# One core, linear attention followed by a highway layer: tokens on partitions to the output, row sums and bias as products, one load form, and an order from a list scheduler

## The chip, the cores and the metric

The kernel runs on 1 core of one Trainium2 chip. The metric is the device time in microseconds; the time before is the median of 3 runs. All reads and writes of HBM, the preparation of the weights and the whole computation lie inside it.

## What is computed

Inputs are q, k and v, each 8 batches x 8 heads x 576 positions x 64 values in float32 (9.4 MB each), two weight matrices of 512 x 512, and a bias of 512. The output is 4608 x 512 in float32 (9.4 MB).

```python
q_s = exp(q - max(q, -1)); q_s /= sum(q_s, -1)        # softmax over the 64 values of a head
k_s = exp(k - max(k, 2));  k_s /= sum(k_s, 2)         # softmax over the 576 positions
kv  = einsum('bhsd,bhse->bhde', k_s, v)               # 64 x 64 for each head
x   = einsum('bhsd,bhde->bhse', q_s, kv)              # then (batch, position) x (head, value) = 4608 x 512
H   = maximum(x @ w_h, 0)
T   = sigmoid(x @ w_t + b_t)
out = T * H + (1 - T) * x
```

Both kernels leave out the subtraction of the maxima: it cancels in the quotient, and the inputs are small (0.1 times a normal draw). Both write the sigmoid as a tanh, T = (1 + tanh(z/2)) / 2[...]. With that, out = x + (1 + tanh(z/2)) (H - x) / 2.

## The kernel before

Two stages run over 8 batches. Positions of a batch are split into a main part of 512 (4 positions on each of 128 partitions, runs of 1 KB in HBM) and a tail of 64 (one position on each of 64 partitions, runs of 256 B). Products have 16-bit inputs.

*Loads* (`load_batch`, L78 to L95). k and q come as float32 through the SyncE queue (L85, L86 and two tails). v comes through GpSimd's queue and is cast to 16 bits on the way: four transfers for the four positions of the main part (L88) and one for the tail (L91). The weights take the same way (L215, L216). Columns of ones are set beside v on VectorE (L92, L93). Each of these tiles has three buffers; batch b+2 is loaded at the end of batch b.

*Prelude* of a batch (L97 to L127). ScalarE takes exp of k and q, main part and tail. VectorE sums exp(q) over each head's 64 values (L112, L113), takes the reciprocal, and multiplies exp(q) by it (L120, L125), all on tiles of 128 x 2048 for the main part. The prelude of batch b+1 is written into batch b behind its first pair of heads.

*Attention*, by pairs of heads (L250 to L286, `flush_rb` L234 to L248). TensorE forms kv for each head of a pair from exp(k) and v, with a column of ones beside v that gives the column sums of exp(k). It transposes the normalised q into PSUM. VectorE takes the reciprocal of the column sums (L279), copies the two 64 x 64 blocks into a block-diagonal 128 x 128 tile (L281 to L283), and scales the transposed q on its way to SBUF (L285). A product (L239, tail L243) gives x with its 512 features on partitions and positions along the free axis; ScalarE copies it into `xT` (L247, L248), which holds all 4608 columns.

*Highway layer*, by chunks of 512 tokens and 128 features (`moe_dc`, L141 to L165). Four products accumulate x W_h and four x W_t, with the weights as the stationary operand. ScalarE takes the tanh, with the bias as a value per partition (L158). VectorE takes dd = max(h, 0) - x (L161), GpSimd uu = dd * tanh (L163), VectorE ww = uu + dd (L172) and gg = 0.5 ww + x (L174). Since features lie on partitions, gg has to be turned: `moe_finish` transposes it on TensorE (L73), ScalarE copies the result to float32 (L191), and the rows are stored through the SyncE queue (L199).

*Order.* The text of the loops sets it: in batch b, each pair of heads is followed by one `moe_dc` of token chunk b-1. Chunks 7 and 8 are done at the end. The tile framework places the waits and may move instructions within its rules; each engine then takes its instructions in a fixed order.

Of the kernel before, what the change touches and what calls it, by code (L numbers as in the profile page):

```python
# [8 lines left out]
FP32 = mybir.dt.float32  # L10
FP16 = mybir.dt.float16
AF = mybir.ActivationFunctionType
ALU = mybir.AluOpType


@with_exitstack
def kernel(
# [10 lines left out]
    nc = tc.nc  # L28
    B, H, S, D = q.shape
    NTOK = B * S  # L30
    DM = H * D
    P = 128
    SM = (S // P) * P
    ST = S - SM
    NPAIR = H // 2
    NJ = SM // P
    KC = DM // P
    assert 0 < ST <= 64

    q_m = q[:, :, 0:SM, :].rearrange("b h (p j) d -> b p h j d", p=P)  # L40
    k_m = k[:, :, 0:SM, :].rearrange("b h (p j) d -> b p h j d", p=P)
    v_m = v[:, :, 0:SM, :].rearrange("b h (p j) d -> b p h j d", p=P)
    q_t = q[:, :, SM:S, :].rearrange("b h p d -> b p h d")
    k_t = k[:, :, SM:S, :].rearrange("b h p d -> b p h d")
    v_t = v[:, :, SM:S, :].rearrange("b h p d -> b p h d")
    w_h_d = moe_w_h.rearrange("(c p) n -> p c n", p=P)
    w_t_d = moe_w_t.rearrange("(c p) n -> p c n", p=P)
    b_t_d = moe_b_t.rearrange("(c p) -> p c", p=P)

    def col_to_row(cg):  # L50
        b_ = cg // S
        u = cg % S
        if u < SM:
            return b_ * S + NJ * (u % P) + (u // P), NJ
        return b_ * S + u, 1

    consts = ctx.enter_context(tc.tile_pool(name="consts", bufs=1))
    xTp = ctx.enter_context(tc.tile_pool(name="xTp", bufs=1))
    qkv = ctx.enter_context(tc.tile_pool(name="qkv", bufs=3))
    ex = ctx.enter_context(tc.tile_pool(name="ex", bufs=2))  # L60
    at_s = ctx.enter_context(tc.tile_pool(name="at_s", bufs=3))
    mo = ctx.enter_context(tc.tile_pool(name="mo", bufs=3))
    gp = ctx.enter_context(tc.tile_pool(name="gp", bufs=5))
    og = ctx.enter_context(tc.tile_pool(name="og", bufs=3))
    ps_qt = ctx.enter_context(tc.tile_pool(name="ps_qt", bufs=2, space=bass.MemoryType.PSUM))
    ps_xt = ctx.enter_context(tc.tile_pool(name="ps_xt", bufs=1, space=bass.MemoryType.PSUM))
    ps_ht = ctx.enter_context(tc.tile_pool(name="ps_ht", bufs=3, space=bass.MemoryType.PSUM))
    ps_nat = ctx.enter_context(tc.tile_pool(name="ps_nat", bufs=2, space=bass.MemoryType.PSUM))

    xT = xTp.tile([P, KC, NTOK], FP16)  # L70

    def ptrans(out_ap, in_ap, idn):
        nc.tensor.matmul(  # L73
            out_ap, in_ap, idn, is_transpose=True, start=True, stop=True,
            skip_group_check=True,
        )

    def load_batch(b):  # L78
        q32m = qkv.tile([P, H, NJ, D], FP32, tag="q32m")
        k32m = qkv.tile([P, H, NJ, D], FP32, tag="k32m")  # L80
        v16m = qkv.tile([P, H, NJ, D + 8], FP16, tag="v16m")
        q32t = qkv.tile([ST, H, D], FP32, tag="q32t")
        k32t = qkv.tile([ST, H, D], FP32, tag="k32t")
        v16t = qkv.tile([P, H, D + 8], FP16, tag="v16t")
        nc.sync.dma_start(k32m, k_m[b])  # L85
        nc.sync.dma_start(q32m, q_m[b])  # L86
        for j in range(NJ):
            nc.gpsimd.dma_start(v16m[:, :, j, 0:D], v_m[b][:, :, j, :])  # L88
        nc.sync.dma_start(q32t, q_t[b])
        nc.sync.dma_start(k32t, k_t[b])  # L90
        nc.gpsimd.dma_start(v16t[0:ST, :, 0:D], v_t[b])  # L91
        nc.vector.memset(v16m[:, :, :, D : D + 8], 1.0)  # L92
        nc.vector.memset(v16t[0:ST, :, D : D + 8], 1.0)  # L93
        nc.vector.memset(v16t[ST:P, :, :], 0.0)
        return q32m, k32m, v16m, q32t, k32t, v16t  # L95

    def prelude(b):  # L97
        q32m, k32m, v16m, q32t, k32t, v16t = loaded[b]
        eq16m = ex.tile([P, H, NJ, D], FP16, tag="eq16m")
        eq16t = ex.tile([ST, H, D], FP16, tag="eq16t")  # L100
        ek16m = ex.tile([P, H, NJ, D], FP16, tag="ek16m")
        ek16t = ex.tile([P, H, D], FP16, tag="ek16t")
        nc.scalar.activation(ek16m, k32m, AF.Exp)  # L103
        nc.scalar.activation(ek16t[0:ST], k32t, AF.Exp)
        nc.scalar.activation(eq16m, q32m, AF.Exp)  # L105
        nc.scalar.activation(eq16t, q32t, AF.Exp)
        nc.vector.memset(ek16t[ST:P], 0.0)
        eqm_g = eq16m.rearrange("p h j d -> p (h j) d")
        qsm = at_s.tile([P, H * NJ], FP16, tag="qsm")
        qst = at_s.tile([ST, H], FP16, tag="qst")  # L110
        with nc.allow_low_precision("fp16 softmax denominators (64 summands)"):
            nc.vector.reduce_sum(qsm, eqm_g, axis=mybir.AxisListType.X)  # L112
            nc.vector.reduce_sum(qst, eq16t, axis=mybir.AxisListType.X)  # L113
        rqm = at_s.tile([P, H * NJ], FP32, tag="rqm")
        rqt = at_s.tile([ST, H], FP32, tag="rqt")
        nc.vector.reciprocal(rqm, qsm)
        nc.vector.reciprocal(rqt, qst)
        qs16m = ex.tile([P, H, NJ, D], FP16, tag="qs16m")
        qs16t = ex.tile([P, H, D], FP16, tag="qs16t")
        nc.vector.tensor_mul(  # L120
            qs16m.rearrange("p h j d -> p (h j) d"),
            eqm_g,
            rqm.broadcast_to([P, H * NJ, D]),
        )
        nc.vector.tensor_mul(qs16t[0:ST], eq16t, rqt.broadcast_to([ST, H, D]))  # L125
        nc.vector.memset(qs16t[ST:P], 0.0)
        return ek16m, ek16t, qs16m, qs16t  # L127

    moe_state = {}

    def moe_start(tcn):
        moe_state[tcn] = {
            "nat": [
                ps_nat.tile([P, 2 * DM], FP16, tag="nat", name=f"nat_{tcn}_{i}")
                for i in range(2)
            ],
            "gg": [],
            "pend": [],
        }

    def moe_dc(tcn, dc):  # L141
        st = moe_state[tcn]
        tok = slice(tcn * 512, (tcn + 1) * 512)
        dsl = slice(dc * P, (dc + 1) * P)
        psh = ps_ht.tile([P, 512], FP32, tag="ht")
        pst = ps_ht.tile([P, 512], FP32, tag="ht")
        for kc in range(KC):
            nc.tensor.matmul(  # L148
                psh, w16h[:, kc, dsl], xT[:, kc, tok],
                start=(kc == 0), stop=(kc == KC - 1),  # L150
            )
        for kc in range(KC):
            nc.tensor.matmul(  # L153
                pst, w16t[:, kc, dsl], xT[:, kc, tok],
                start=(kc == 0), stop=(kc == KC - 1),
            )
        th = mo.tile([P, 512], FP16, tag="th")
        nc.scalar.activation(th, pst, AF.Tanh, bias=bt2[:, dc : dc + 1], scale=0.5)  # L158
        xs = xT[:, dc, tok]
        dd = mo.tile([P, 512], FP16, tag="dd")  # L160
        nc.vector.scalar_tensor_tensor(dd, psh, 0.0, xs, op0=ALU.max, op1=ALU.subtract)  # L161
        uu = mo.tile([P, 512], FP16, tag="uu")
        nc.gpsimd.tensor_mul(uu, dd, th)  # L163
        moe_flush_pend(tcn)
        st["pend"].append((dd, uu, xs, dc))  # L165

    def moe_flush_pend(tcn):
        st = moe_state[tcn]
        while st["pend"]:
            dd, uu, xs, dc = st["pend"].pop(0)  # L170
            ww = mo.tile([P, 512], FP16, tag="ww")
            nc.vector.tensor_add(ww, uu, dd)  # L172
            gg = gp.tile([P, 512], FP16, tag="gg")
            nc.vector.scalar_tensor_tensor(gg, ww, 0.5, xs, op0=ALU.mult, op1=ALU.add)  # L174
            st["gg"].append((gg, dc))

    def moe_finish(tcn):
        st = moe_state.pop(tcn)
        nats = st["nat"]
        for gg, dc in st["gg"]:  # L180
            for t in range(4):
                ptrans(
                    nats[t // 2][
                        :, (t % 2) * DM + dc * P : (t % 2) * DM + (dc + 1) * P
                    ],
                    gg[:, t * P : (t + 1) * P],
                    ident,
                )
        for half in range(2):
            o32 = og.tile([P, 2, DM], FP32, tag="o32")  # L190
            nc.scalar.copy(o32.rearrange("p a b -> p (a b)"), nats[half])  # L191
            for tt in range(2):
                c0 = tcn * 512 + half * 256 + tt * P
                i = 0
                while i < P:
# [24 lines left out]
    for _ in range(34):  # L220
        ptrans(warm[:, 0:P].bitcast(FP16)[:, 0:P], ident, ident)
# [3 lines left out]
    for b in range(B):  # L225
        ek16m, ek16t, qs16m, qs16t = pre.pop(b)
        _, _, v16m, _, _, v16t = loaded[b]
        if b > 0:
            moe_start(b - 1)
# [109 lines left out]
```

The softmax here doesn't subtract the row's maximum and nothing guards it: scores larger than these inputs give would overflow.

## Time and profile before

| what | value |
|---|---|
| time, median of 3 runs | 222.03 us (221.61 to 222.95) |
| span of the profiled run | 219.1 us, 3271 instructions |
| HBM read, written | 30.41 MB, 9.44 MB |
| DMA packets | 69696, 34.29 MB as written |

The profile gives the busy time of each engine over the span, the same in 40 equal slices (a digit is tenths of a slice), the DMA queues, and the chain of work that ended last. "hardware_dynamic" is the queue of the transfers that SyncE issues, "software_dynamic" of those that GpSimd issues. Groups of instructions are given by line, engine, operation and shapes, with count, busy time and mean; then the idle time of the engine just before them and what ended it. Overlapping matmuls make TensorE's busy time an upper measure of its work. [...]

### The profile page before, as it was taken

The page shows a single profiled execution, that of the slowest core. Times are in us where ns is not written, and L with a number is a line of the kernel's source. Part 1 is how long each engine was busy: PE and PEld are TensorE (multiplying, and loading weights), DVE is VectorE, ACT ScalarE, POOL GpSimd, SP SyncE. Part 2 cuts the span into 40 slices and gives each one's busy share as a digit, 9 for nine tenths or more (in the row PEclk, how much of TensorE's full clock was granted, in tenths as well). Part 3 has the DMA queues.
Part 4 walks back from the last instruction along what each step waited for, and adds up shares of the span by engine and source line. Part 5 has one row for each costly group of instructions (what it writes and reads, how often), then busy time and mean ns, then how long its engine had stood idle before and what let it go on. Part 6 is the DMA issues. An engine that isn't in the chain of part 4 may idle for free.

```text
span 219.1 us, 3271 instructions
## 1 busy us (share of the span) xinstructions
PE 137.4 (63%) x1170; PEld 71.3 (33%) x1170; DVE 164.5 (75%) x357; ACT 102.0 (47%) x151; POOL 79.5 (36%) x84
## 2 busy tenths in 40 slices
PE   4110573029768553894799299939965899878420
PEld 4110441014334221542354045415522455334210
DVE  3074595009993899699979997999999999878820
ACT  2443344603676423783667464607532275535230
POOL 8532311231566304650294049222402434452600
PEclk9855558556999797699589959985996999999955
DMA  6999999999999999997899209920060033071426
GB/s 185 253 211 268 210 249 252 229 270 223 274 221 186 127 280 223 283 112 160 262 254 162 93 0 73 183 47 0 3 193 3 0 120 74 0 195 50 141 56 135
DMA packets 69696, 34.29 MB, mean 157 GB/s; under 512 B 47664, under 2 KB 65072, under 8 KB 69680
## 3 DMA queue, kind: packets, MB, share of 16 engines
q1 hardware_dynamic: 31120, 28.32, 50.4%
q0 software_dynamic: 38560, 5.77, 37.2%
q8 instruction: 9, 0.15, 0.3%
q14 instruction: 7, 0.06, 0.1%
HBM read 30.41 MB, written 9.44 MB: 182 GB/s over the span
## 4 chain that ended last, share of the span: by engine, by line
DVE 38%; DMA 30%; issue 13%; POOL 9%; PE 4%; ACT 2%; ACTq 1%; POOLq 0%; DVEq 0%
DMA v16m<-in_v_dram 30%; DVE gg L174 9%; POOL uu L163 5%; DVE dd L161 5%; DVE qsm L112 5%; DVE ww L172 5%; DVE qsT L285 4%; POOL v16m L88 3%; DVE qs16t L125 2%; DVE abk L283 2%; DVE qst L113 1%; DVE rz L279 1%; PE qtt L73 1%; DVE abk L282 1%; PE nat L73 1%
## 5 line engine op out<-in xcount | busy, mean ns | idle before, releaser
L163 POOL TENSOR_TENSOR uu<-dd,th 128x512 f16<-128x512 f16 x36 | 43.3, 1205 | 79.1 <-DVE dd L161 66.1
L153 PE MATMUL pst<-xT,w16t 128*128 128x512 f16 x144 | 44.8, 415 | 17.7 <-DVE dd L161 17.2
L148 PE MATMUL psh<-xT,w16h 128*128 128x512 f16 x144 | 42.2, 395 | 5.5 <-ACT th L158 3.5
L88 POOL DMA_DIRECT2D v16m<-in_v_dram x32 | 28.9, 906 | 37.1 <-DMA v16m<-in_v_dram 19.0
L158 ACT ACTIVATE th<-pst,bt 128x512 f16<-128x512 f32 x36 | 24.9, 691 | 32.5 <-PE pst L153 32.5
L174 DVE SCALAR_TENSOR_TENSOR gg<-ww,xT 128x512 f16<-128x512 f16 x36 | 34.8, 966 | 0.3
L247 ACT CAST xT<-pxT 128x512 f16<-128x512 f32 x32 | 18.7, 583 | 27.7 <-PE qtt L243 27.5
L260 PE MATMUL qtt<-v16m,ek16m 128*64 128x65 f16 x256 | 17.6, 224 | 22.2 <-DMA v16m<-in_v_dram 21.4
L260 PEld LDWEIGHTS <-ek16m 128*64 128x64 f16 x256 | 12.4, 129 | 41.3 <-issue 41.1
L112 DVE TENSOR_REDUCE qsm<-eq16m 128x32 f16<-128x2048 f16 x8 | 18.2, 2277 | 9.8 <-ACT eq16m L105 9.7
L172 DVE TENSOR_TENSOR ww<-uu,dd 128x512 f16<-128x512 f16 x36 | 18.7, 520 | 9.0 <-POOL uu L163 8.7
L153 PEld LDWEIGHTS <-w16t 128*128 128x128 f16 x144 | 13.7, 102 | 35.0 <-issue 23.7
L105 ACT ACTIVATE eq16m<-q32m 128x2048 f16<-128x2048 f32 x8 | 15.3, 1907 | 21.0 <-DMA q32m<-in_q_dram 9.3
L161 DVE SCALAR_TENSOR_TENSOR dd<-psh,xT 128x512 f16<-128x512 f32 x36 | 23.9, 664 | 1.1 <-PE psh L148 1.0
L73 PE MATMUL nat<-ident,gg 128*128 128x128 f16 x144 | 16.3, 245 | 12.8 <-DVE gg L174 12.5
L191 ACT CAST o<-nat 128x1024 f32<-128x1024 f16 x18 | 17.4, 1016 | 12.9 <-PE nat L73 12.9
L73 PE MATMUL qtt<-ident,qs16m 128*64 128x128 f16 x256 | 22.5, 258 | 0.0
L103 ACT ACTIVATE ek16m<-k32m 128x2048 f16<-128x2048 f32 x8 | 15.4, 1920 | 13.2 <-DMA k32m<-in_k_dram 12.6
L279 DVE RECIPROCAL rz<-qtt 128x1 f32<-128x1 f32 x32 | 5.2, 162 | 20.0 <-PE qtt L73 19.8
L239 PE MATMUL pxT<-qsT,abk 128*128 128x512 f16 x32 | 14.9, 465 | 6.5 <-ACT xT L247 3.7
L148 PEld LDWEIGHTS <-w16h 128*128 128x128 f16 x144 | 13.2, 100 | 17.3 <-issue 6.3
L285 DVE TENSOR_SCALAR qsT<-qtt,rz 128x640 f16<-128x640 f16 x32 | 17.6, 550 | 1.0
(38 smaller groups left out, 170.8 us busy)
## 6 DMA issues: line engine op xcount, KB each, us to landing
k32m<-in_k_dram SPq DMA_DIRECT2D x8, 1024.0 KB, 12.5
q32m<-in_q_dram SPq DMA_DIRECT2D x8, 1024.0 KB, 14.2
out_dram<-o SPq DMA_DIRECT2D x40, 128.0 KB, 2.4
v16m<-in_v_dram POOLq DMA_DIRECT2D x32, 128.0 KB, 10.2
out_dram<-o SPq DMA_DIRECT2D x16, 256.0 KB, 2.7
q32t<-in_q_dram SPq DMA_DIRECT2D x8, 128.0 KB, 11.4
k32t<-in_k_dram SPq DMA_DIRECT2D x8, 128.0 KB, 10.3
v16t<-in_v_dram POOLq DMA_DIRECT2D x8, 64.0 KB, 11.2
```

The lines of the kernel that those rows point to most:

```text
L73: nc.tensor.matmul(out_ap, in_ap, idn, is_transpose=True, start=True, stop=True, skip_group_check=True,)
L88: nc.gpsimd.dma_start(v16m[:, :, j, 0:D], v_m[b][:, :, j, :])
L112: nc.vector.reduce_sum(qsm, eqm_g, axis=mybir.AxisListType.X)
L148: nc.tensor.matmul(psh, w16h[:, kc, dsl], xT[:, kc, tok], start=(kc == 0), stop=(kc == KC - 1),)
L153: nc.tensor.matmul(pst, w16t[:, kc, dsl], xT[:, kc, tok], start=(kc == 0), stop=(kc == KC - 1),)
L158: nc.scalar.activation(th, pst, AF.Tanh, bias=bt2[:, dc : dc + 1], scale=0.5)
L161: nc.vector.scalar_tensor_tensor(dd, psh, 0.0, xs, op0=ALU.max, op1=ALU.subtract)
L163: nc.gpsimd.tensor_mul(uu, dd, th)
L172: nc.vector.tensor_add(ww, uu, dd)
L174: nc.vector.scalar_tensor_tensor(gg, ww, 0.5, xs, op0=ALU.mult, op1=ALU.add)
L260: nc.tensor.matmul(psk[od, :], ek16m[:, h, j, :], v16m[:, h, j, 0 : D + 1], start=(j == 0), stop=False,)
L285: nc.vector.tensor_scalar_mul(qsT, pqt, rz)
```

## The change

The kernel is rewritten. What it computes stays.

*Layout and loads.* A batch now has 64 groups of 9 consecutive positions, so a head and group is one run of 9 x 64 values, 2304 B. Partition (hh, p) holds group p of head 2c + hh. q, k and v have the same form, all come as float32 through the SyncE queue, in 2 parts per batch (k and v of batch 0 in 4), with three buffers each. GpSimd casts v to 16 bits beside a set column of ones. The weights come as float32 too and are cast on the core: W_t on ScalarE, W_h on VectorE.

*Attention.* kv is formed for two pairs of heads and both halves of the partitions. VectorE writes it, divided by the column sums, into 128 x 130 blocks: block-diagonal with two heads, 65 columns each, of which the last holds ones. exp(q) is transposed without being normalised. The product of it with such a block has tokens on partitions (128 tokens: 2 positions of each of 64 groups), and its column 64 is the row sum of exp(q). VectorE divides by it on the way out of PSUM and writes x in 16 bits, tokens on partitions.

*Highway layer.* There are 36 tiles of 128 tokens. x is transposed (4 transposes, ScalarE copies the result), and is now the stationary operand; the weights are what moves, 512 columns. The bias is a fifth product, of a row of ones with the bias, split into a 16-bit value and its remainder. W_h is stored as (W_h - I)/2, so that the product is (h - x)/2. tanh is taken in place in PSUM; d = max(-x/2, (h - x)/2); u = (tanh + 1) d, both on VectorE with one operand in PSUM; o = u + x on GpSimd, to float32; two stores of 64 rows.

*Order.* `Plan` holds each step with its engine, a length, a key and what it needs, and limits from the number of buffers. It goes through time and on each engine takes, of the steps that are ready, the one with the smallest key (a due time; the highway steps are due 2.9 us apart per tile, the others count back from their users). The resulting order is what is written, and the framework keeps it (`manual_schedule`). Loads are held back so that a bounded amount of transfer is outstanding. xu (also used by kv, two banks), the transposed q and the transposed x have one PSUM buffer each, the two wide products two each.

The core of the diff, which replaces the whole kernel:

```diff
-        for j in range(NJ):
-            nc.gpsimd.dma_start(v16m[:, :, j, 0:D], v_m[b][:, :, j, :])
...
-            nc.vector.reduce_sum(qsm, eqm_g, axis=mybir.AxisListType.X)
...
-        nc.vector.tensor_mul(
-            qs16m.rearrange("p h j d -> p (h j) d"),
...
-        th = mo.tile([P, 512], FP16, tag="th")
-        nc.scalar.activation(th, pst, AF.Tanh, bias=bt2[:, dc : dc + 1], scale=0.5)
...
-        nc.gpsimd.tensor_mul(uu, dd, th)
...
-            nc.scalar.copy(o32.rearrange("p a b -> p (a b)"), nats[half])
...
+LEN = dict(
+    mm=216, bias=216, qt=480, qt8=120, xu=250, xt=240, kv=1050, xu9=300, warm=2400,
+    expk=1240, expk1=700, expq=1120, expq8=400, th=690, xe=560, wcast_t=1900, qc=1000, qc8=350,
+    xs=850, kvn=1000, dd=660, uu=660, wcast=1150, wdiag=900, small=200,
+    vcast=1250, vcast1=650, oo=1220,
+    dma=60, lag=150, backlog=6000, spare=800, start=15500, tile=2900,
+)
...
+                    can = [
+                        s for s in pools[eng]
+                        if ready_at[s.name] <= now
+                        and all(free[t] > 0 for t in s.takes)
+                        and (not s.paced or fabric - now < LEN["backlog"])
+                    ]
+                    if not can:
+                        continue
+                    s = min(can, key=lambda s: s.key)
...
+    ps_t = pool("ps_t", 2, space=PS)
+    ps_g = pool("ps_g", 2, space=PS)
+    ps_x = pool("ps_x", 1, space=PS)
+    ps_q = pool("ps_q", 1, space=PS)
+    ps_xt = pool("ps_xt", 1, space=PS)
...
+        src = source[which][b].rearrange("(c hh) (p j) d -> (hh p) c (j d)", hh=2, p=NP)[:, c0:c0 + n]
...
+    def vcast(b, c, n):
+        nc.gpsimd.tensor_copy(
+            v16[b % NV][:, c:c + n, :, 0:D], T[f"v32{b}"][:, c:c + n].rearrange("p c (j d) -> p c j d", j=NJ))
...
+        for kk in range(2):
+            for j in range(NJ):
+                for half_ in range(2):
+                    rows = slice(64 * half_, 64 * half_ + 64)
+                    nc.tensor.matmul(
+                        ps[:, half_, kk * 130:kk * 130 + 130].rearrange("p (w e) -> p w e", w=2),
+                        ek[rows, j, 2 * kk:2 * kk + 2].rearrange("p c d -> p (c d)"), vv[rows, 2 * kk:2 * kk + 2, j, 0:65],
+                        start=(j == 0), stop=(j == NJ - 1), skip_group_check=True,
...
+        copy = nc.scalar.copy if on_act(g) else nc.vector.tensor_copy
...
+            copy(e, ps.rearrange("p (a s) c -> p a c s", s=2))
...
+                nc.tensor.matmul(dst, T[f"eq{b}_{jp // 2}"][:, jp % 2, n], kvb[b % NKV][:, half_, kk],
+                                 start=True, stop=True, skip_group_check=True)
...
+        nc.vector.reciprocal(rs, z[:, :, :, 64])
...
+        nc.vector.tensor_mul(x, z[:, :, :, 0:64], rs.unsqueeze(3).to_broadcast([P, 2, 4, D]))
...
+            nc.tensor.matmul(T[f"tps{i}"], T[f"xT{i}"][:, n], wt16[:, n], start=(n == 0), stop=False,
+                             skip_group_check=True)
+        else:
+            nc.tensor.matmul(T[f"tps{i}"], ones, b16, start=False, stop=True, skip_group_check=True)
...
+        nc.tensor.matmul(T[f"gps{i}"], T[f"xT{i}"][:, n], wh16[:, n], start=(n == 0), stop=(n == 3),
+                         skip_group_check=True)
...
+        nc.scalar.activation(T[f"tps{i}"], T[f"tps{i}"], AF.Tanh, scale=0.5)
...
+        nc.vector.scalar_tensor_tensor(d, T[f"x{i}"], -0.5, T[f"gps{i}"], op0=ALU.mult, op1=ALU.max)
...
+        nc.vector.scalar_tensor_tensor(t, T[f"tps{i}"], 1.0, T[f"d{i}"], op0=ALU.add, op1=ALU.mult)
...
+        nc.gpsimd.tensor_add(o, T[f"u{i}"], T[f"x{i}"])
...
+            nc.sync.dma_start(dst[:, 2 * jp + half_], T[f"o{i}"][half_::2])
...
+    order = plan.order()
+    with tc.manual_schedule():
+        for _, s in order:
+            s.emit()
```

## Prediction

> **What bounds the kernel now.** I read the page first, parts 1, 2 and 4, for which engine is full and where.
>
> ```profile
> PE 137.4 (63%) x1170; PEld 71.3 (33%) x1170; DVE 164.5 (75%) x357; ACT 102.0 (47%) x151; POOL 79.5 (36%) x84
> DVE  3074595009993899699979997999999999878820
> PEclk9855558556999797699589959985996999999955
> DMA  6999999999999999997899209920060033071426
> DVE 38%; DMA 30%; issue 13%; POOL 9%; PE 4%; ACT 2%; ACTq 1%; POOLq 0%; DVEq 0%
> ```
>
> No engine is full on average, but two stages show. In the first 17 slices (5.5 us each, to about 93 us) DMA stands at 9 and DVE does not; after slice 22 DMA falls away and DVE stands at 9. The chain says the same: 30% DMA, then 38% DVE. The queue part and the windows tell why the transfers are slow (columns of a window: length, busy us of PE, PEld, DVE, ACT, POOL, granted clock, DMA share, GB/s).
>
> ```profile
> q1 hardware_dynamic: 31120, 28.32, 50.4%
> q0 software_dynamic: 38560, 5.77, 37.2%
> 3.00:6.00 3.00, 3.00 (x32) 3.00 (x31) 0.00 (x0) 0.00 (x0) 3.00 (x5) 1.00 1.01 339
> 10.00:25.00 15.00, 3.26 (x40) 2.83 (x41) 7.31 (x13) 5.41 (x5) 4.19 (x5) 0.50 1.42 231
> 145.00:160.00 15.00, 13.32 (x110) 6.98 (x110) 14.49 (x38) 8.70 (x14) 4.71 (x4) 0.77 0.05 11
> 175.00:190.00 15.00, 14.20 (x132) 7.32 (x132) 14.25 (x35) 8.18 (x16) 5.62 (x5) 1.00 0.25 71
> ```
>
> The software queue carries v and the weights, casting on the way: 38560 packets of 150 B each take 37.2% of 16 engines' span for 5.77 MB, three quarters of what the other queue takes for 28.32 MB. In 10-25 us they move 231 GB/s together, and TensorE, waiting, runs at clock 0.50. From 145 us DMA is at 0.05 and DVE at 14.49 of 15 us: VectorE is the bound. The groups show on what.
>
> ```profile
> L174 DVE SCALAR_TENSOR_TENSOR gg<-ww,xT 128x512 f16<-128x512 f16 x36 | 34.8, 966 | 0.3
> L161 DVE SCALAR_TENSOR_TENSOR dd<-psh,xT 128x512 f16<-128x512 f32 x36 | 23.9, 664 | 1.1 <-PE psh L148 1.0
> L172 DVE TENSOR_TENSOR ww<-uu,dd 128x512 f16<-128x512 f16 x36 | 18.7, 520 | 9.0 <-POOL uu L163 8.7
> L120 DVE TENSOR_TENSOR qs16m<-eq16m,rqm 128x2048 f16<-128x2048 f16 x8 | 18.3, 2291 | 0.0
> L112 DVE TENSOR_REDUCE qsm<-eq16m 128x32 f16<-128x2048 f16 x8 | 18.2, 2277 | 9.8 <-ACT eq16m L105 9.7
> L285 DVE TENSOR_SCALAR qsT<-qtt,rz 128x640 f16<-128x640 f16 x32 | 17.6, 550 | 1.0
> 201.03 1.03 PE L148 MATMUL psh<-xT,w16h 128*128 128x512 f16 x4
> 201.90 1.03 PE L153 MATMUL pst<-xT,w16t 128*128 128x512 f16 x4
> ```
>
> The last two are from the timeline (start, length): at full clock four 512-column products start 0.87 us apart, so 0.217 us each. The page's 395 to 415 ns is not their price, since they overlap.
>
> [...] gg, two SBUF inputs, took 625 to 1853 ns, dd, one of them in PSUM, only 626 to 692. [...] the trace has 339 in 3-6 us beside the small packets.
>
> **The change, part by part.**
>
> *Loads.* All three inputs come by the hardware queue in rows of 2304 B; v's cast moves to GpSimd. Packets: 28.3 MB / 2304 + 1024 weight rows + 4608 output rows = about 17,900 for 69,696. Bytes through the engines: 30.4 + 9.4 = 39.9 MB. The rate is not shown alone. From below: queue 1 moved 28.32 MB in 50.4% of 219.1 us, 256 GB/s, with 1 KB and 256 B packets; from above the 339 of 3-6 us[...]. I take 339, for the packets are larger: 118 us for all.
>
> *VectorE.* Out go qsm, qs16m and their tails, both abk casts, qsT, ww and gg: 18.2 + 5.3 + 18.3 + 6.4 + 13.8 + 17.6 + 18.7 + 34.8 = 133 us. Per 128-token tile there are now a reciprocal (as rz, 0.16) and three 512-element instructions with a PSUM input, xs, dd and uu (as dd, median 0.68): 2.2 us, by 36 = 79. No VectorE instruction of the loop has two SBUF inputs any more, so GpSimd stretches none. Per batch: the copy of 1024 transposed values (between 550 x 1024/640 = 0.88 and qs16m's 1.12 ns per element, 1.15; I take 1.15[...]), one of 256 (0.3), the kv normalisation (2 x 0.16 + 2 x 0.4 = 1.1): 2.55, by 8 = 20. Setup 6. Sum 106 us, from 164.5.
>
> *TensorE.* Per tile 4 + 4 products and one for the bias, 9 x 0.217 = 1.95; four for x and its row sums (130 columns) and four transposes at 0.057 each (the trace's nat: eight in 0.61 us, one 0.22, so 0.39/7): 0.46. Sum 2.41, by 36 = 87. Per batch 18 transposes of q, 1.03, and 36 products for kv, alternating between row halves: 36 x 0.057 = 2.05 if one after another, 1.03 if the halves run together[...]. I take 1.03. Sum 103 us, up to 111. The transposes of the output are gone; the bias costs 36 x 0.217 = 7.8 and relieves nothing that binds.
>
> *ScalarE.* From th (0.69) and a 512 copy (0.58): 1.27 by 36 = 46. Exp from 1910 ns for 2048 and 620 for 512: 0.84 ns per element + 0.19: 2 x 1.16 + 2 x 1.05 + 0.40, and a 1024 copy 1.02 (as o): 5.8 by 8 = 47. Sum 96 with the weight cast. The casts to o32 leave.
>
> *GpSimd.* 36 sums at 1.16 (uu's median) = 42; v casts of 1152 elements 16 times, between 1.2 ([...]a shade over the ScalarE time)[...] hidden under the others.
>
> *Waits.* One buffer each for xu, xtps and the transposed q: the next xu, queued in order on TensorE, waits for xs, and with it every product behind it. The loop of one buffer is 0.23 + 0.16 + 0.68 + three hops of 0.1, 1.4 us of a 2.9 us tile, so it fits if neither engine is late. Stores and loads share one queue: a load stands behind a store that waits for GpSimd, but the order puts the loads about two batches ahead.
>
> *The sum.* Before the first wide product, k, q, v and w_t must land: 4.6 MB / 339 = 13.6, + 0.7 for the first issue, 2 for the landing, 2.1 for the cast, about 1 for hops and queueing: 19.5 us. By then TensorE has done batch 0's kv and q (3 us), VectorE about 8: both have about 100 us left. The bound engine ran at 95 to 97% in the windows from 145 us. Here two are within 3% of each other in a fixed order and wait on single buffers, so neither can lead; 0.97 is the upper end, 0.80 the lower, and I take 0.90: 111 us. After the last product dd's and uu's followers: a sum 1.2, issue 0.6, landing 2.4, hops and end, about 6. Span 19.5 + 111 + 6 = 136.5; the times lie 2.9 above the span (222.0 to 219.1): 139.
>
> **Rivals.**
> *DMA sets the pace.* v of batch 7 lands after all loads and 20 tiles' stores, 35.6 MB: at 339 at 107 us, then cast, kv, its normalisation, the first tile's fill (7.5), five tiles (14.5), tail 6 and 2.9: 138, no loss. At 300 it lands at 121, and the end is at 152; at 256, 172. For it: some windows of pure stores show only 203 GB/s at share 0.94. Against: packets twice as large, none of the software queue.
> *The fixed order stalls.* Efficiency 0.80: 19.5 + 125 + 6 + 2.9 = 153. For it: single buffers. Against: the loop of 1.4 us.
> *TensorE stays at half clock.* 103 us become 206, less 6 done early: 19.5 + 200 + 6 + 2.9 = 228, slower than 222. For it: 0.50 in every starved stage of before. Against: 1.00 wherever work came densely, and now its share of busy is near 0.9.
>
> **How the numbers follow.** Forecast 0.62, DMA 0.20, stalls 0.15, half clock 0.03. Low end: efficiency 0.97 and a start 1 us earlier, 19.5 - 1 + 103 + 6 + 2.9 = 130, less 3 if instructions pack at 0.60 as dd and gg do in the timeline: 127. High end past the two slow cases: 157. Faster by over 1%: 0.96; within 1%: 0.01; slower: 0.03.
>
> **What would show it.** Right: software queue gone, mean over 300 GB/s while loading; 512-element VectorE rows at 0.65 to 0.70 with no long ones; TensorE's clock 1.00 from 20 us on; wide products 2.9 to 3.2 us apart per tile; VectorE near 105 us busy. Wrong: first wide product after 24 us, DMA at 9 through 110 us, xu waiting on xs for long, or ScalarE or GpSimd as what is waited for.

## Result and the profile after

The changed kernel takes 139.25 us (median; 138.85 to 139.52) beside 221.82 us (220.39 to 222.95) for the kernel before in the same session. The ratio is 0.6278, 95% interval 0.6245 to 0.6312. The forecast was 139.0 us. In two of the runs below some executions took over 1.5% longer than the fastest of the same kernel, two of four with both edits together and one of four of the kernel before with v by the hardware queue; the times and ratios given leave them out.

The page of the changed kernel, parts 1 to 4:

```profile
PE 116.2 (85%) x1084; PEld 68.4 (50%) x1084; DVE 103.4 (75%) x216; ACT 86.8 (63%) x125; POOL 60.8 (44%) x62
DVE  5025169578879798988899889989898899897640
PEclk9999999999999999999999999999999999999996
DMA  4999999999999999989999999999962241223233
q1 hardware_dynamic: 19940, 39.86, 80.7%
PE 69%; DVE 13%; DMA 5%; issue 4%; POOL 2%; SPq 2%; ACT 1%; POOLq 1%; DVEq 0%; ACTq 0%
```

The software queue is gone, with its 38560 packets. DMA still stands at 9 in nearly all of the first 29 slices, but it has left the chain, where it falls from 30% to 5%. TensorE has taken the chain over, at 69%, with VectorE far behind in share. The window of the steady stretch shows how near VectorE is all the same (columns as before, PE to POOL with instruction counts in brackets, then clock, DMA share, GB/s):

```profile
40.00:130.00 90.00, 89.06 (x849) 50.92 (x847) 79.03 (x156) 61.39 (x93) 46.67 (x41) 1.00 0.77 274
```

TensorE is busy for 9.9 us of 10, VectorE for 8.8. TensorE's figure is an upper measure: the record of a wide product is 0.38 us long, where the next one starts 0.22 us later. Two of VectorE's groups in the loop:

```profile
L487 DVE SCALAR_TENSOR_TENSOR d<-x,gps 128x512 f16<-128x512 f16 x36 | 24.7, 686 | 7.3 <-PE gps L478 6.5
L492 DVE SCALAR_TENSOR_TENSOR u<-tps,d 128x512 f16<-128x512 f32 x36 | 24.8, 688 | 2.9
```

These two replace dd, ww and gg. The 36 u lie between 679 and 693 ns, so the spread of gg (625 to 1853) has gone.

The clock line shows full rate from the start, and this is the one line of the page that misleads. TensorE's timeline of the same execution (start, length):

```profile
11.19 1.04 PE L406 MATMUL qps<-idh,qe 128*128 128x128 f16 x8 [6.58 <-ACT qe L397]
14.49 2.13 PE L360 MATMUL kv<-v,ek 64*128 64x130 f16 x36
21.71 1.91 PE L470 MATMUL tps<-wt,xT 128*128 128x512 f16 x4
26.49 1.03 PE L470 MATMUL tps<-wt,xT 128*128 128x512 f16 x4
31.59 1.21 PE L360 MATMUL kv<-v,ek 64*128 64x130 f16 x36
```

The same 36 products of kv take 2.13 us at 14.49 and 1.21 us at 31.59; the same four wide products 1.91 and 1.03. Until about 25.5 us TensorE runs at half its rate, after an idle time of 6.58 us ahead of the first q transposes. The record of the granted clock does not contradict this. In the trace its first entry, 1.00, begins at 26.0 us, and the page shows a stretch without an entry as full. Another kernel, the one with the tanh in SBUF, has entries from early on. Its products are spaced as here (2.13 us for the first 36 of kv, 1.91 for the first four wide ones), and its record changes where the spacing does:

```profile
8.30:25.20 16.90, 9.53 (x84) 6.80 (x85) 8.77 (x20) 8.93 (x12) 2.66 (x4) 0.50 1.05 389
25.40:30.00 4.60, 4.12 (x28) 2.14 (x27) 3.10 (x6) 4.13 (x6) 2.12 (x2) 1.00 1.05 391
```

The DMA share of 1.05, which the changed kernel has too (1.05 from 30 to 40 us), comes without a software queue, so a share a little above 1 needs none; in 10 to 25 us of the kernel before, with both queues at work, it is 1.42. As for the clock, a mean of the record depends on where its entries begin. Four executions of the changed kernel, with spans of 137.1 to 137.7 us, have means of 0.992, 0.928, 0.927 and 0.974. Missing early entries would explain these, but only the first of the four has a trace, so for the others this is not shown.

By the forecast's own parts, the span of 137.4 us is 21.7 to the first wide product (forecast 19.5), 109.1 to the end of the last one (111), and a tail of 6.6 (6). The time lies 1.7 us above the span (2.9). The four differences, +2.2, -1.9, +0.6 and -1.2, add up to -0.3.

### The profile page after: what moved, and what is told of

Read it like the earlier page. It is cut to its first block, busy times and chain, and to the rows that moved or that the text cites. A ratio compares the mean times of both kernels' runs of the same rounds, so it can differ in the third digit from the quotient of the medians.

```text
span 137.4 us, 2961 instructions
## 1 busy us (share of the span) xinstructions
PE 116.2 (85%) x1084; PEld 68.4 (50%) x1084; DVE 103.4 (75%) x216; ACT 86.8 (63%) x125; POOL 60.8 (44%) x62
## 2 busy tenths in 40 slices
DMA packets 19954, 40.04 MB, mean 291 GB/s; under 512 B 2018, under 2 KB 2018, under 8 KB 19940
## 3 DMA queue, kind: packets, MB, share of 16 engines
q1 hardware_dynamic: 19940, 39.86, 80.7%
## 4 chain that ended last, share of the span: by engine, by line
PE 69%; DVE 13%; DMA 5%; issue 4%; POOL 2%; SPq 2%; ACT 1%; POOLq 1%; DVEq 0%; ACTq 0%
PE tps L470 20%; PE gps L478 19%; PE xu L443 8%; PE qps L406 6%; PE kv L360 6%; PE xtps L458 5%; DMA q<-in_q_dram 5%; PE tps L473 5%; DVE x L452 3%; DVE eq L418 3%; POOL o L497 2%; DVE d L487 2%; DVE u L492 2%; DVE kvb L374 2%; SPq L240 2%
## 5 line engine op out<-in xcount | busy, mean ns | idle before, releaser
L497 POOL TENSOR_TENSOR o<-u,x 128x512 f32<-128x512 f16 x36 | 41.6, 1155 | 57.3 <-DVE u L492 45.9
L470 PE MATMUL tps<-wt,xT 128*128 128x512 f16 x144 | 38.0, 386 | 0.7 <-ACT xT L464 0.7
L478 PE MATMUL gps<-wh,xT 128*128 128x512 f16 x144 | 37.9, 384 | 0.0
L482 ACT ACTIVATE tps<-tps 128x512 f32<-128x512 f32 x36 | 21.0, 583 | 23.6 <-PE tps L473 23.3
L487 DVE SCALAR_TENSOR_TENSOR d<-x,gps 128x512 f16<-128x512 f16 x36 | 24.7, 686 | 7.3 <-PE gps L478 6.5
L492 DVE SCALAR_TENSOR_TENSOR u<-tps,d 128x512 f16<-128x512 f32 x36 | 24.8, 688 | 2.9
L452 DVE TENSOR_TENSOR x<-xu,rs 128x512 f16<-128x512 f32 x36 | 24.9, 691 | 2.1
L464 ACT COPY xT<-xtps 128x512 f16<-128x512 f16 x36 | 21.1, 587 | 7.4 <-PE xtps L458 6.9
L397 ACT ACTIVATE qe<-q 128x1024 f16<-128x1024 f32 (+1 forms) x24 | 19.6, 840 | 1.2 <-DMA q<-in_q_dram 1.2
L478 PEld LDWEIGHTS <-xT 128*128 128x128 f16 x144 | 13.2, 99 | 11.5 <-issue 0.6
L470 PEld LDWEIGHTS <-xT 128*128 128x128 f16 x144 | 12.9, 99 | 11.7 <-ACT xT L464 0.9
```

Source lines behind the costliest of these rows:

```text
L452: nc.vector.tensor_mul(x, z[:, :, :, 0:64], rs.unsqueeze(3).to_broadcast([P, 2, 4, D]))
L464: nc.scalar.copy(t, T[f"xtps{i}"])
L470: nc.tensor.matmul(T[f"tps{i}"], T[f"xT{i}"][:, n], wt16[:, n], start=(n == 0), stop=False, skip_group_check=True)
L478: nc.tensor.matmul(T[f"gps{i}"], T[f"xT{i}"][:, n], wh16[:, n], start=(n == 0), stop=(n == 3), skip_group_check=True)
L482: nc.scalar.activation(T[f"tps{i}"], T[f"tps{i}"], AF.Tanh, scale=0.5)
L487: nc.vector.scalar_tensor_tensor(d, T[f"x{i}"], -0.5, T[f"gps{i}"], op0=ALU.mult, op1=ALU.max)
```

## Experiments

My theory: TensorE sets the pace with VectorE close behind, in an order that keeps both fed, and transfers are hidden. The rivals: DMA sets the pace; VectorE does, and TensorE only looks full; the order's waits do. A further group of runs takes parts of the change away. Each time stands beside 139.25 us. The runs come from three other sessions, in which the kernel before took 221.07, 221.39 and 221.70 us beside 221.82 here, so half a microsecond says nothing. Except for the two runs on the order of kv and of the whole, the scheduler makes a new order from the edited steps, so a change of 1 or 2 us can also come from that.

### Without the bias product

Leaves out the bias: 36 products of 512 columns, by the forecast's step 36 x 0.217 = 7.8 us of TensorE.

```diff
-        for n in range(5):
+        for n in range(4):
```

> The bias product of each tile is left out (the sum x W_t has no bias), 36 products of 512 columns at 0.217 us, 7.8 us of TensorE; nothing else changes. My theory now, TensorE alone sets the pace from 21 to 131 us: 139.25 - 7 to 8, so 131 to 133. Rival, VectorE sets it together with TensorE (88% busy): at most half of that, 135 to 138. Rival, DMA sets it (9 in every slice to 100 us): 138 to 140.

Measured: 136.51 us (135.87 to 137.89), ratio 0.6173 (0.6128 to 0.6217). Of 7.8 us only 2.7 come back, which is in the range of the first rival and not of my theory. The chain of this kernel, from its page, and then its window next to that of the changed kernel:

```profile
DVE 45%; PE 27%; issue 8%; DMA 5%; ACT 5%; POOL 3%; SPq 2%; POOLq 1%; DVEq 0%; ACTq 0%
```

```profile
60.00:110.00 50.00, 48.44 (x502) 29.44 (x502) 46.08 (x93) 37.37 (x56) 28.29 (x25) 1.00 0.87 316
```

```profile
60.00:110.00 50.00, 49.60 (x490) 28.57 (x487) 44.19 (x88) 37.28 (x56) 28.36 (x25) 1.00 0.88 317
```

VectorE rises from 44.19 to 46.08 of 50 us and takes the chain. TensorE's waits between 22 and 130 us tell the same (who waited for whom: us in total, times, longest). The largest of this kernel, and then all that are listed of the changed kernel:

```profile
PE xu L443 <- DVE x L452: 2.2, 3, 1.2
PE kv L360 <- DVE x L452: 1.2, 3, 0.6
```

```profile
PE tps L470 <- ACT xT L464: 0.7, 1, 0.7
PE xu L443 <- DVE x L452: 0.5, 1, 0.5
```

All listed waits together grow from 1.2 to 5.8 us, 4.4 of them for VectorE, and this is most of the time that does not come back. So TensorE did set the pace, and VectorE stood some 3 us behind.

### The transposed q copied by ScalarE

ScalarE takes two of the three copies of a batch, and not one: 8 copies of 1.22 us leave VectorE.

```diff
-        return g == 1
+        return g < 2
```

> The copy of the first 1024 transposed q values of a batch moves from VectorE (8 x 1.22 us) to ScalarE (8 x 1.01 us). Theory, TensorE sets the pace: 138 to 140, or 1 to 2 us less if its waits for x come from a late VectorE. Rival, VectorE sets it: 130 to 133. Rival, ScalarE has no room: over 141.

Measured: 141.02 us (140.43 to 141.14), ratio 0.637 (0.6336 to 0.6403). VectorE falls to 94.9 us busy, ScalarE rises to 93.8, and nothing is gained. The window:

```profile
40.00:130.00 90.00, 88.40 (x847) 50.33 (x844) 72.21 (x149) 66.33 (x97) 45.19 (x41) 1.00 0.74 273
```

VectorE has 18 us free in 90 and TensorE is about as full as before. VectorE alone is not the bound. But the edit is no pure relief, since ScalarE takes the work over: the time lies at the lower edge of the third expectation, "ScalarE has no room". TensorE's waits between 22 and 130 us, 3.1 us where the changed kernel has 1.2, grow by as much as the time does. Half of them are for ScalarE, and half for x, which comes late in spite of the free time:

```profile
PE xu L443 <- DVE x L452: 1.5, 2, 0.8
PE tps L470 <- ACT xT L464: 0.9, 1, 0.9
PE xtps L458 <- ACT xT L464: 0.7, 1, 0.7
```

### Both together

> Both of two earlier edits: no bias product (the sum x W_t has no bias; 7.8 us of TensorE) and the first q copy on ScalarE (9.8 us of VectorE, 8.1 us more on ScalarE). Alone they gave 136.5 and 141.0 against 139.25. Theory, TensorE and VectorE are within a few per cent of each other and the later one sets the pace: relieved together they give what neither gives alone, 131 to 134. Rival, what was left over in the first is latency of the fixed order and not VectorE's load: 136 to 138. Rival, ScalarE becomes the bound: over 138.

Leaves out the bias too. Measured: 133.2 us (133.08 and 133.31), ratio 0.6011 (0.5955 to 0.6068). The window:

```profile
40.00:120.00 80.00, 79.55 (x806) 47.74 (x804) 69.00 (x146) 64.54 (x97) 44.03 (x40) 1.00 0.84 304
```

Relief of VectorE, worth nothing alone, is worth 3.3 us once TensorE is relieved. The chain goes back to TensorE (59%; ScalarE 11%, VectorE 10%). Two engines a few us apart is what these three runs show, the one that leads being TensorE. The third rival, the waits of the order, has no run of its own. Of the 7.8 us taken from TensorE 6.0 come back here. What holds the other 1.8, and what keeps TensorE in the changed kernel at 0.92 to 0.93 of its own prices (worked out below), stays open.

### v of two batches only

Leaves out the loads and casts of v for batches 2 to 7, which use those of the first two: 7.1 MB and 13 us of GpSimd less.

```diff
-            for which in "kqv":
+            for which in ("kqv" if b < NV else "kq"):
```

> v is loaded and cast for batches 0 and 1 only; batches 2 to 7 use what those left, so 7.1 MB of 39.9 and 12 of GpSimd's 18 casts are left out. Theory, TensorE sets the pace and the loads are hidden though DMA shows 9 up to 100 us: 138 to 140. Rival, the transfers set it: 7.1 MB at 0.36 MB per us is 20 us, 119 to 125.

Measured: 140.61 us (139.42 to 141.12), ratio 0.6342 (0.6299 to 0.6384). No gain, while DMA is mostly free from the 23rd slice on. The 1.4 us more lie ahead of the first wide product, which starts at 23.1 us; from there to the end of the last one it takes 109.3 us, as in the changed kernel (109.1). The line of the page:

```profile
DMA  4999999999999999999999143212331241223233
```

The transfers are hidden, and the waits of SyncE's queue on stores (27.6 us for o, in the changed kernel) cost nothing. The first rival falls.

### kv one row half after the other

The 36 products of a group are the same, in two sets of 18. In each set the nine on partitions 0 to 63 now come first, then the nine on 64 to 127.

```diff
-            for j in range(NJ):
-                for half_ in range(2):
+            for half_ in range(2):
+                for j in range(NJ):
```

> The 36 products of kv come with all nine of one row half first and then all nine of the other, instead of alternating; the same products. In the changed kernel 36 of them take 1.15 us, 0.032 each, although 130 columns need 0.057 at full clock. Theory, two row halves run at once: 36 x 0.057 = 2.05, 0.9 us more for each batch, 7 us in all, 145 to 147 if TensorE sets the pace. Rival, short products pipeline to 0.032 whatever their rows: 139 to 140, and 36 of them still in 1.15 us.

Measured: 142.07 us (141.55 to 142.35), ratio 0.6413 (0.6381 to 0.6444), 2.8 us more. One group in the chain of this kernel (start, length):

```profile
84.38 1.60 PE kv L360 x36
```

1.55 to 1.62 us against 1.14 to 1.22: some 0.4 us in each of 8 batches, 3.2 us, of which 2.8 reach the end. This lies between theory and rival. The halves do run beside each other when they alternate: 1.00 us pass from the first start to the last (below), where 36 x 0.057 is 2.05. That the gain is 1.35-fold and not twofold has its reason in this run: its blocks don't run strictly one after another. Windows on kv alone, from the start of a group, count the products begun so far (length, busy us and count, clock, DMA share, GB/s); first this run, then the changed kernel:

```profile
84.37:84.65 0.28, 0.28 (x5) 1.00 0.89 347
84.37:84.88 0.51, 0.51 (x13) 1.00 0.91 355
```

```profile
82.03:82.31 0.28, 0.27 (x10) 1.00 1.04 393
82.03:82.54 0.51, 0.50 (x18) 1.00 1.01 383
```

Alternating, two products start every 0.057 us, and 1.00 us passes from the first start to the last. In blocks, the first ones start one by one, 0.057 us apart, as priced from the transposes. But at each of the three borders between blocks eight products start in four pairs, a pair every 0.057 us. That makes 24 steps of 0.057, 1.37 us, and 1.39 pass from the first start to the last. The trace doesn't name a product's row half; that a pair is of two halves follows from where it lies. So the forecast's two prices, 0.057 alone and half of that together, both hold.

### The clock kept up

The same computation, with 24 groups of 8 small products into a spare PSUM tile, at the lowest priority, where TensorE has nothing to do before the first wide product.

```diff
+    for f in range(NFILL):
+        add(f"fill{f}", "PE", "qt", 10 ** 9 + f, fill0 if f == 0 else fill, [f"fill{f - 1}" if f else "warm"])
```

> 24 groups of 8 transposes' worth of products on a spare bank fill TensorE's idle time until the first wide product; the computation is the same. In the changed kernel the products of 11 to 25.5 us start at the distance of the half clock (eight transposes 1.05 us, later 0.45; kv 2.08, later 1.15; four wide ones 1.71, later 0.86) although the granted clock is shown as 1.00. Theory, the array was at half clock there after 6.5 idle us: those stand at their later values, the first wide product comes 1 to 2 us earlier and the time is 2 to 4 us less, 135.5 to 137.5. Rival, these products were slow because their operands came late: no change, 139 to 140, or a little more for fillers in the way.

Measured: 137.33 us (137.2 to 138.03), ratio 0.6207 (0.6159 to 0.6255), 1.9 us less. The interval just touches that of the changed kernel, so the place of the gain counts. TensorE's timeline:

```profile
14.26 1.39 PE L373 MATMUL kv<-v,ek 64*128 64x130 f16 x36
19.92 1.04 PE L483 MATMUL tps<-wt,xT 128*128 128x512 f16 x4 [0.23 <-ACT xT L477]
```

Against 2.13 and 1.91 in the changed kernel. The clock record of this trace has its first entry, 1.00, at 5.3 us and not at 26.0. The first wide product comes 1.8 us earlier: so much of the 2.2 us by which the start was late is the half rate. From there to the end of the last product both kernels take about 109.1 us.

### The order as written

The same steps and buffers, put down batch by batch and tile by tile, where the changed kernel has the scheduler's order.

```diff
-    order = plan.order()
+    def whole(i):
+        put(f"xu{i}", f"xs{i}", f"xt{i}", f"xe{i}", *[f"mt{i}_{n}" for n in range(5)], f"th{i}",
+            *[f"mh{i}_{n}" for n in range(4)], f"dd{i}", f"uu{i}", f"oo{i}", f"st{i}_0", f"st{i}_1")
...
+    order = seq_
```

> The same steps, buffers and layout, but the order is batch by batch and tile by tile, each tile from its first product to its store before the next, and the next batch's preparation before the third tile; the scheduler's order is not used. Theory, the order is what lets TensorE run at 95%: each tile then waits for x (1.1), for the copy of its transpose (0.8) and for d and u of the tile before (1.5) with nothing else in the queue, 5 to 6 us a tile and 3 to 5 more a batch: 215 to 255, no better than before. Rival, the operations and the loads carry the gain and buffers hide the order: 145 to 165.

Measured: 378.62 us (376.98 to 379.33), ratio 1.7076 (1.6965 to 1.7187). It is far over what I expected, and slower than the kernel before. One tile in the timelines of VectorE and TensorE (start, length, and idle time ahead):

```profile
203.90 0.69 DVE L487 SCALAR_TENSOR_TENSOR d<-x,gps 128x512 f16<-128x512 f16 x1 [4.93 <-PE gps L478]
211.21 0.69 DVE L487 SCALAR_TENSOR_TENSOR d<-x,gps 128x512 f16<-128x512 f16 x1 [4.96 <-PE gps L478]
```

```profile
206.31 0.40 PE L458 MATMUL xtps<-idh,x 128*128 128x128 f16 x4 [2.12 <-DVE x L452]
207.44 1.89 PE L470 MATMUL tps<-wt,xT 128*128 128x512 f16 x4 [0.73 <-ACT xT L464]
```

A tile takes 7.31 us, and it is one loop: VectorE's x of a tile stands in its queue behind d and u of the tile before, which wait for that tile's products; the products of this tile wait for x. VectorE and TensorE take turns. With 4.9 us idle per tile on one and 2.9 on the other, TensorE is at the low clock for most of the time: in the record 3.4 us of 1.00 alternate with 0.50, which lasts up to 23.9 us, and the mean is 0.67. The nine wide products of this tile take 3.6 us (207.44 to 211.0) where 1.95 do at full rate. So some 1.6 us of its 7.31 is the clock, and 36 such loops are 263 of the 379 us; the rest is the start and the preparations of batches, each of which adds 10 to 11 us. My expectation had too little for both, and left the clock at full rate.

### v by the casting queue

v comes as before, cast on the way by GpSimd's queue, into the new layout.

```diff
-        nc.gpsimd.tensor_copy(
-            v16[b % NV][:, c:c + n, :, 0:D], T[f"v32{b}"][:, c:c + n].rearrange("p c (j d) -> p c j d", j=NJ))
+        for cc in range(c, c + n):
+            nc.gpsimd.dma_start(v16[b % NV][:, cc, :, 0:D], src[:, cc])
```

> v comes as before the change, cast on the way by GpSimd's queue (36864 packets of 256 B read), straight into its 16-bit tile; all else, the scheduler too, is as changed. GpSimd's casts fall away. Theory, the load form was half of the early bound: the small packets cost about 78 us of all 16 engines, as before, beside 30 MB of others at 0.36 MB per us, 84 us, so the DMA is full to 150 us or so: 160 to 185. Rival, the queues overlap well enough to hide it behind TensorE: 139 to 146.

Measured: 162.2 us (161.12 to 163.22), ratio 0.7319 (0.7262 to 0.7376), 23 us more. TensorE's timeline of this kernel shows where:

```profile
22.62 1.16 PE L359 MATMUL kv<-v,ek 64*128 64x130 f16 x18 [6.72 <-DMA v<-in_v_dram]
31.81 1.16 PE L359 MATMUL kv<-v,ek 64*128 64x130 f16 x18 [8.04 <-DMA v<-in_v_dram]
```

v of the first batch is late twice, and the first wide product starts at 40.3 us, 18.6 later than in the changed kernel; 4.6 us come after that. The time fell where I expected it, but not for the reason that I gave: the casting transfers delay the first batch, they don't keep DMA the bound to the end. The run doesn't separate the small packets from the fact that v of two batches is asked for at once, eight transfers from 1.76 us on.

### The kernel before with v by the hardware queue

The other way round: only the load form of v is put into the kernel before, with one buffer for v in float32 and the cast on GpSimd.

```diff
-        for j in range(NJ):
-            nc.gpsimd.dma_start(v16m[:, :, j, 0:D], v_m[b][:, :, j, :])
+        nc.sync.dma_start(v32m, v_m[b])
...
+        nc.gpsimd.tensor_copy(v16m[:, :, :, 0:D], v32m)
```

> The kernel before with one part of the change: v comes as float32 through SyncE's queue and GpSimd casts it to 16 bits; the weights keep their casting transfers. Layout, products and the written order are the old ones. If the early stage of before was bound by the small packets of the software queue, its first 93 us shrink until VectorE binds there too: 164.5 us busy at 0.93 to 0.97 plus a start of about 10 and an end of about 8 give 188 to 200 us. If the casts (8 of 128x2048 at 2 to 2.4 us and 8 tails, some 20 us on GpSimd, whose uu VectorE waits for) or the waits of the written order take its place, it stays at 205 to 222 us. A time above 225 would say that the load form was no burden for the kernel before at all.

Measured: 209.25 us (207.0 to 209.26), ratio 0.9408 (0.9347 to 0.9469). That is in the second of the expected ranges and not in the first. The window of 25 to 60 us of this kernel, from an execution of 211.31 us, and then of the kernel before:

```profile
25.00:60.00 35.00, 24.96 (x222) 12.79 (x220) 30.61 (x69) 19.31 (x29) 11.63 (x8) 0.79 0.88 240
```

```profile
25.00:60.00 35.00, 18.34 (x142) 8.81 (x142) 21.30 (x45) 14.98 (x22) 9.73 (x11) 0.64 1.40 246
```

VectorE goes from 21.30 to 30.61 us of 35: the casting transfers did hold it back, and with them gone it is the fullest engine from 25 us on. From there to 200 us it is busy 156 us of 175, 0.89, where I had taken 0.93 to 0.97. So the load form of v alone brings 12.5 of the 82.6 us. A first stage that was full of DMA for 93 us had VectorE close behind it. That the rest comes from the work taken off VectorE (164.5 us busy before, 103.4 after), in an order that keeps it and TensorE fed, is argued from these figures; no run puts VectorE's old steps back into the changed kernel.

### The tanh in SBUF

One operand of u moves from PSUM to SBUF, so that both lie in SBUF. This tests the step "GpSimd stretches none".

```diff
-        nc.scalar.activation(T[f"tps{i}"], T[f"tps{i}"], AF.Tanh, scale=0.5)
+        t = dp.tile([P, DM], FP16, tag="t16", name=f"t16_{i}")
+        nc.scalar.activation(t, T[f"tps{i}"], AF.Tanh, scale=0.5)
```

> The changed kernel with one edit: the tanh goes to a 16-bit tile in SBUF and not back into its PSUM bank, so that u = (tanh + 1) d has two SBUF inputs. If two SBUF inputs beside GpSimd stretch a VectorE instruction, as gg of the kernel before suggests (mean 966 ns, 625 to 1853), u grows from 688 ns toward 850 to 970, 36 of them add 6 to 10 us to VectorE, which has only some 0.5 to 1 us in 10 free beside TensorE: 142 to 147 us. If PSUM inputs are no protection, or the scheduled order keeps GpSimd and u apart, u stays within 5% of 688 ns and the time is 138 to 140 us; the bank of the tanh comes free earlier, which could even give 1 us.

Measured: 142.4 us (141.51 to 143.03), ratio 0.6435 (0.6406 to 0.6464), 3.1 us more. The timelines of VectorE, GpSimd and TensorE around the longest u:

```profile
53.51 1.67 DVE L494 SCALAR_TENSOR_TENSOR u<-t,d 128x512 f16<-128x512 f16 x1
56.75 0.69 DVE L494 SCALAR_TENSOR_TENSOR u<-t,d 128x512 f16<-128x512 f16 x1
```

```profile
53.49 1.14 POOL L349 CAST v<-v 128x1152 f16<-128x1152 f32 x1
```

```profile
56.17 1.22 PE L360 MATMUL kv<-v,ek 64*128 64x130 f16 x36 [1.12 <-DVE x L452]
```

32 of the 36 u keep 0.68 to 0.70 us. The four others, 0.84, 1.02, 1.67 and 1.54, are those that overlap a GpSimd instruction by 0.3 us or more, three a cast of v and one a sum o, and each is the overlap plus 0.55 us: 53.51 to 54.63 is 1.12, plus 0.55 is 1.67. Five more meet only the last 0.04 to 0.15 us of one, and overlap plus 0.55 then comes to no more than their usual length. So u waits until GpSimd is done. In the changed kernel, with one operand in PSUM, seven of the 36 u overlap a GpSimd instruction by 0.2 to 0.7 us, and none is lengthened. The delayed x then makes TensorE wait for the single xu buffer (1.12 us here, 0.90 after the u of 1.54); its waits from 22 us on are 4.3 us, 3.1 more than in the changed kernel. Neither of my two sizes was right: the effect is there, up to 1.67 us for 0.69, but the order lets only four of 36 meet it for long, 2.3 us on VectorE.

### A shorter end, with the clock kept up

The filler products, and for the last tile the sum o on VectorE and its second store from ScalarE's queue.

```diff
-        nc.gpsimd.tensor_add(o, T[f"u{i}"], T[f"x{i}"])
+        (nc.vector if i == len(tiles) - 1 else nc.gpsimd).tensor_add(o, T[f"u{i}"], T[f"x{i}"])
```

> The changed kernel with the filler products before the first wide product (as in e6_clock_kept_up) and a shorter end: the last tile's sum o runs on VectorE, idle by then, and its second store is issued by ScalarE. The sum on GpSimd took 1155 ns where VectorE takes about 0.7, and the second issue no longer stands behind the first (about 0.6 us): 0.5 to 1.1 us less than the fillers alone, so 136.2 to 136.9 us. If the last landing does not depend on the second issue, or VectorE has u of that tile late, it stays at 137.3 +- 0.4.

Measured: 136.74 us (136.35 to 137.15), ratio 0.617 (0.6149 to 0.6192). That is within what I expected, and faster than both kernels: its interval lies below that of the changed kernel. Beside the fillers alone it is 0.6 us less, which the intervals of those two can't tell from nothing, though o took 0.69 us in place of 1.15 in the trace.

## Why the prediction was right, step by step

*The sum.* Right to 0.3 us, with terms that partly cancel: that it is as close as this is luck, since three of the four terms were 1 to 2 us off. The start was 2.2 us late because the early products ran at half rate; the forecast had TensorE's first 3 us of work at full rate, although its own evidence, 0.50 in the starved stage of before, spoke against that. The run with fillers gives 1.8 us of it back. The stretch from first to last wide product took 109.1 for 111, less by an efficiency that was mis-sized: by the forecast's prices TensorE had 36 x 2.41 + 7 x 2.06, less 1 done early, about 100 us of work there, so 100/109.1 = 0.92, and about 0.93 without the slow first 4 us, where I had taken 0.90. The tail was 0.6 too short, the difference of time and span 1.2 too long. Where time and span are of one execution they are 1.7 to 1.8 us apart, in the kernel before too (139.13 and 137.4, 221.57 and 219.8); the forecast's 2.9 set a median time beside the span of another execution.

*"Neither can lead."* This is the part of the argument that failed. TensorE does lead: it has 69% of the chain, relief of it alone brings 2.7 us, and relief of VectorE alone, at ScalarE's cost, brings nothing. The other half, two engines within 3%, holds: after 2.7 of the 7.8 us of the bias, VectorE takes over.

*VectorE.* The forecast adds up lengths, so its 106 us stands beside 109.4, the sum of the recorded lengths; consecutive ones overlap a little in the record, and the busy time is 103.4. The 512-element instructions took 0.686 to 0.691 for 0.68, the copy of 1024 1.22 where I took 1.15 (the upper price, 1.12 ns per element, was itself a little low), the reciprocal 0.20 for 0.16. That GpSimd stretches none is right for u (679 to 693 ns), and was worth 3 us here: with the tanh in SBUF four u took 0.84 to 1.67 us. One reading of the kernel before was too simple: "DMA stands at 9 and DVE does not" in the first 17 slices, where VectorE's line has six nines. The run with v by the hardware queue shows how near VectorE was.

*TensorE.* kv took 1.00 from first start to last, for the 1.03 chosen of 1.03 to 2.05 (its 1.14 to 1.22 include the recorded length of the last product). That choice was an assumption, with no figure of the kernel before to show it. The loop of the one xu buffer took 1.42 us where it is tight (xu at 102.55, the next at 103.97), for 1.4: hops of 0.03 to 0.05 where I assumed 0.1, and a recorded 0.40 for four products of xu where I took 0.23; the wide products 0.217 as priced. "Relieves nothing that binds" was right of the bias product, but its price in time is 2.7 us and not 7.8.

*ScalarE and GpSimd.* ScalarE's recorded lengths add up to 92.7 for 96, and with their overlaps to 86.8 us busy: the tanh with a plain factor took 0.583 us and not the 0.69 of the form with a bias operand, 3.9 us in all. GpSimd was busy for 60.8 us, and 36 x 1.16 + 16 x 1.2 is 61.0: the v cast of 1152 elements took 1.145, a little below my 1.2, which was an estimate from ScalarE's time. Both hidden, as said.

*Loads.* 358 to 404 GB/s in most slices while loading, above the 339 taken; done by about 100 us. Packets 19,940 for 17,900: 2018 of them have 4 B, which is 126 x 16 + 2, beside 126 transfers of 128 KB or more and two of 2 KB. The DMA rival, 152 us, was refuted by leaving 7.1 MB out.

*The rivals of order and clock.* Neither came, but both are real: the written order gives them together, 378.6 us. The forecast weighed the clock rival with the share of busy time, and this was the right thing to look at, though its "1.00 wherever work came densely" is not what its own line for 145 to 160 us says (13.32 of 15 us busy, 0.77), nor is its "0.50 in every starved stage" what 100 to 104 us has (1.17 of 4 us busy, 1.00). What keeps the share high is the order: the same instructions in the written order have a mean clock of 0.67.

*What would show it.* All held, but for one: the clock was not at full rate from 20 us, but from about 25.5. A tile took (130.8 - 25.5)/35 = 3.0 us with its share of the batch work, inside 2.9 to 3.2.

## What to carry to other kernels

Where two engines are a few us apart, price an edit by how far the next engine is behind, not by what it removes: 7.8 us off the leader brought 2.7, and some 9 us moved from the second to a third engine nothing, until both were done. An order in which one tile's late steps stand ahead of the next tile's early ones in an engine's queue can turn the engines into a relay: in the written order a tile took 7.31 us for 3.0, and TensorE, idle for 2.9 us of them, had a mean clock of 0.67, so that the two losses came together. Judge the clock by the spacing of products of one shape, early against late: the page's clock line shows full rate also where the trace has no entry (here up to 26.0 us).

## What was not expected of the hardware

- TensorE started its work at half rate, 6.58 us after the last of its first 24 products, and kept to it for some 14 us, in which it was often idle. The clock record of that trace begins only at 26.0 us. In the run with the tanh in SBUF it reads 0.50 from 8.2 to 25.3 us, with the same spacing of products.
- 192 small products in idle time were enough to keep the rate up through a start of 20 us: kv 1.39 for 2.13 us, the first four wide products 1.04 for 1.91.
- With both inputs of u in SBUF, the four u that overlapped a GpSimd instruction by 0.3 us or more (a cast of 1.14 us, a sum of 1.15, neither of them longer than usual) took the overlap plus 0.55 us: 0.84, 1.02, 1.67 and 1.54 for the usual 0.69. With one input in PSUM seven overlapped one by 0.2 to 0.7 us, and none took over 0.693.
- 36 products on alternating row halves started in pairs, one every 0.057 us, 1.00 us from first start to last. In blocks of nine, products started singly every 0.057 us, except that at each border of blocks eight of them still started in four pairs: 1.39 us from first start to last.
